# One table of steps in a new order: linear attention and a gated projection on one core

## The chip, the core and the metric

The kernel runs on one core of one Trainium2 chip, in one launch. The metric is the device time of one execution in microseconds (us); a figure for a kernel is the median of three timed runs. The engines of the core are named as in the profile: PE (TensorE, the matrix products), PEld (its weight loads), DVE (VectorE), ACT (ScalarE), POOL (GpSimd) and SP (SyncE, which issues the transfers).

## The reference

There are 8 batches of 8 heads, 576 tokens and 64 features. The first half is linear attention, the second a projection with a gate from a convolution over time:

```python
q_s = exp(q - max(q, -1));  q_s = q_s / (sum(q_s, -1) + 1e-09)   # over features
k_s = exp(k - max(k, 2));   k_s = k_s / (sum(k_s, 2) + 1e-09)    # over tokens
kv  = einsum('bhsd,bhse->bhde', k_s, v)
x   = einsum('bhsd,bhde->bhse', q_s, kv)      # -> [8, 576, 512]
xp  = x with 4 rows of zeros ahead of the tokens
gate = sigmoid(sum over k < 5 of conv_w[k] * xp[:, k:k+576, :])
out  = (gate * (x @ w_val)) @ w_out
```

## The kernel before, in words

Each batch goes through the same stages; steps of several batches interleave. A step is a small function with a name, a batch and mostly a slab, that is 128 of the 512 channels (0 to 3): `value 4 1` is the product with w_val of batch 4, output slab 1. A letter at the end of a step names its engine: a for ACT, v for DVE, p for POOL. Steps without a letter have a fixed engine.

- **k.** `load_km`, `k_peak` (DVE, L271), `k_row` and `k_spread` (transfers) find the maximum of each channel; `k_sub` (L286) takes it off in five pieces, `k_exp` (ACT, L290 and L291) raises them. Batches 0 and 1 have k by channels (`k_top`, `k_raise`) and turn it on PE. `kv` (PE, L393) forms k'v, `kv_norm` (L403 to L411) divides, `kv_high` and `kv_low` (L419) split it into a rounded upper part and the rest.
- **q.** `q_max` (DVE, L343), `q_sub` (L347), `q_exp` (ACT, L351), `q_sum` (DVE, L358 to L360) and `q_mul` (L378 on ACT in eight small instructions, L380 elsewhere), the last three in parts. `q_turn` (PE, L425) transposes q, `q_turned` copies it, `q_low` (DVE, L435) keeps the rest.
- **x.** `attend` (PE, L458, L459) gives a slab of x in PSUM. `x_high` copies its upper part, `x_low` (DVE, L478) the rest; `first` (L472 on ACT, L474 on DVE) and four `tap` steps build the gate from the same PSUM tile. A tap is one instruction on DVE (L484), or a product on ACT (`far`, L487) and a sum on POOL (L488). `sigmoid` (ACT, L491) ends the gate.
- **products.** `value` (PE, L502) multiplies all four slabs of x with one slab of w_val, 24 matmuls with upper and lower parts; `gated` (DVE, L523) makes g, `g_high` and `g_low` (L531) split it; `project` (PE, L502) does the same with w_out, and `store` copies the result from PSUM and sends it out (L545).
- **weights.** `part`, `field`, `scaled`, `signed`, `joined`, `w_high` and `w_low` turn the 64-bit words of w_val (slabs 0 to 3) and w_out (4 to 7) and of the taps (8) into upper and lower parts of 32 bits.

What sets the order is written out by hand: the table ORDER (lines 32 to 134) holds 893 steps, and a loop calls them one after the other. Each engine works off its own steps in this order and waits, in order, for what they need; nothing is moved by a planner. The PSUM tiles come from two pools of two buffers each: `x` (x and the turned q) and `mm` (kv, values, products). So the third tile of a pool waits until one of the two before it has been read for the last time: an `attend` waits for the taps and `x_low` of an earlier one, a `project` for a `store`. `warm 0` issues nothing.

Of the kernel before, what the change touches and what calls it, by code (L numbers as in the profile page):

```python
# [47 lines left out]
    attend 0 2, w_high 3 a, w_low 3 p, first 0 2 a, tap 0 2 3 v, w_high 2 a, tap 0 2 2 a, x_high 0 2 a, attend 0 3,
    load_km 2 1, warm 0, first 0 3 a, signed 4, x_high 0 3 a, w_low 2 p, kv_norm 1 a, part 4 a, sigmoid 0 0,
    x_low 0 2, x_low 0 3, value 0 0, load_q 2, scaled 5 a, load_v 2, tap 0 3 3 v, q_mul 1 0 p, tap 0 2 1 v,  # L50
    q_mul 1 3 p, tap 0 3 2 v, tap 0 2 0 v, joined 4 p, gated 0 0, value 0 2, k_peak 2 1, sigmoid 0 2, tap 0 3 1 v,
    g_high 0 0 a, gated 0 2, value 0 1, w_high 4 a, q_mul 1 1 p, sigmoid 0 1, signed 5, g_high 0 2 a, field 7,
    load_km 2 0, field 6, q_turn 1 0, g_low 0 2 v, g_low 0 0 p, value 0 3, tap 0 3 0 v, part 5 a, q_max 2, w_low 4 p,
    sigmoid 0 3, load_km 2 3, gated 0 1, k_peak 2 0, q_turned 1 0 a, joined 5 p, q_turn 1 1, w_high 5 p, scaled 6 a,
    w_low 5 p, gated 0 3, scaled 7 a, q_turned 1 1 a, k_peak 2 3, g_high 0 1 a, g_high 0 3 a, attend 1 0, attend 1 1,
    first 1 0 a, signed 7, first 1 1 a, x_high 1 0 a, signed 6, q_sub 2 2 p, g_low 0 3 v, q_sub 2 0 p, g_low 0 1 p,
    tap 1 0 3 v, part 6 a, tap 1 0 2 v, project 0 0, load_q 3, joined 6 p, tap 1 1 3 a, x_low 1 0, w_high 6 a,
    x_high 1 1 a, project 0 1, warm 0, tap 1 0 1 v, tap 1 0 0 v, k_row 2, attend 1 3, load_k 3, w_low 6 p,
    load_km 3 0, q_sub 2 3 v, part 7 a, load_km 3 1, tap 1 1 2 v, q_sub 2 4 p, store 0 0 a, tap 1 1 1 v, store 0 1 a,
    project 0 2, joined 7 p, k_spread 2, tap 1 1 0 v, first 1 3 a, x_low 1 1, x_high 1 3 a, w_high 7 a, q_sub 2 1 p,  # L60
    attend 1 2, sigmoid 1 1, store 0 2 a, w_low 7 p, k_sub 2 0 p, sigmoid 1 0, project 0 3, q_max 3, x_high 1 2 a,
    k_sub 2 3 p, tap 1 3 3 v, x_low 1 3, k_sub 2 1 p, tap 1 3 2 v, x_low 1 2, k_peak 3 1, k_sub 2 2 p, load_km 4 2,
    q_exp 2, first 1 2 a, tap 1 3 1 v, value 1 0, store 0 3 a, q_sum 2, gated 1 0, tap 1 2 3 v, load_km 3 3,
    k_peak 3 3, k_sub 2 4 p, value 1 1, k_peak 3 0, q_mul 2 4 p, load_v 4, k_exp 2, load_km 3 2, gated 1 1,
    q_mul 2 3 p, kv 2, tap 1 3 0 v, q_mul 2 0 a, sigmoid 1 3, g_high 1 0 p, g_low 1 0 p, q_mul 2 1 p, value 1 3,
    tap 1 2 2 v, kv_norm 2 a, q_mul 2 2 p, k_peak 3 2, kv_high 2 a, tap 1 2 1 v, q_turn 2 0, q_turned 2 0 a,
    load_km 4 0, k_row 3, g_high 1 1 a, tap 1 2 0 v, q_sub 3 1 p, sigmoid 1 2, gated 1 3, q_sub 3 3 p, kv_low 2 p,
    g_low 1 1 p, k_peak 4 0, q_turn 2 1, g_high 1 3 a, tail_turn 2, warm 0, q_sub 3 2 p, q_turned 2 1 v, g_low 1 3 p,
    q_low 2 0, value 1 2, tail_turned 2 a, k_spread 3, q_low 2 1, gated 1 2, attend 2 1, g_high 1 2 p, first 2 1 v,
    g_low 1 2 p, tap 2 1 3 v, q_sub 3 0 p, load_q 4, k_sub 3 0 p, attend 2 0, project 1 3, k_peak 4 2, x_high 2 0 a,  # L70
    k_sub 3 1 p, first 2 0 a, k_sub 3 3 p, load_k 4, load_km 5 1, tap 2 1 2 v, load_km 4 3, load_km 5 3, tap 2 1 1 v,
    project 1 1, q_exp 3, load_v 3, x_high 2 1 a, k_sub 3 2 p, x_low 2 0, tap 2 0 3 v, k_peak 5 1, store 1 3 a,
    load_km 4 1, store 1 1 a, x_low 2 1, project 1 0, k_sub 3 4 p, warm 0, tap 2 1 0 a, tap 2 0 2 v, tap 2 0 1 v,
    attend 2 2, k_exp 3, store 1 0 a, tap 2 0 0 a, first 2 2 a, kv 3, q_sum 3, x_high 2 2 a, attend 2 3, k_peak 4 1,
    first 2 3 a, q_max 4, q_mul 3 1 p, tap 2 3 3 a, project 1 2, q_mul 3 3 p, kv_norm 3 v, k_peak 5 3, tap 2 2 3 v,
    kv_high 3 p, tap 2 3 2 a, x_low 2 2, x_high 2 3 a, q_mul 3 2 p, load_km 7 3, q_sub 4 1 p, x_low 2 3, tap 2 2 2 v,
    q_sub 4 0 p, sigmoid 2 1, tap 2 2 1 v, load_km 5 0, value 2 1, k_peak 4 3, kv_low 3 v, store 1 2 a, q_mul 3 0 a,
    tap 2 2 0 v, load_km 6 3, value 2 2, sigmoid 2 2, q_turn 3 0, gated 2 1, tap 2 3 1 v, q_sub 4 3 p, q_turned 3 0 a,
    gated 2 2, tap 2 3 0 v, k_row 4, q_low 3 0, g_high 2 2 a, q_sub 4 2 p, load_v 6, value 2 0, k_peak 6 3,
    g_high 2 1 a, sigmoid 2 0, g_low 2 2 v, q_turn 3 1, load_q 5, gated 2 0, attend 3 0, q_sub 4 4 p, k_spread 4,  # L80
    q_turned 3 1 a, sigmoid 2 3, first 3 0 v, q_low 3 1, load_km 6 2, g_low 2 1 p, tap 3 0 3 v, value 2 3, q_exp 4,
    g_high 2 0 p, g_low 2 0 p, x_high 3 0 a, gated 2 3, attend 3 1, k_peak 5 0, load_km 5 2, g_high 2 3 v,
    tap 3 0 2 v, first 3 1 a, x_low 3 0, tap 3 0 1 v, load_kt 4, k_peak 6 2, g_low 2 3 p, x_high 3 1 a, tap 3 1 3 a,
    tap 3 1 2 a, x_low 3 1, tap 3 0 0 v, project 2 3, k_sub 4 3 v, project 2 0, attend 3 3, q_sum 4, tap 3 1 1 a,
    store 2 3 a, k_peak 5 2, k_sub 4 0 p, tap 3 1 0 a, x_high 3 3 a, k_sub 4 4 p, warm 0, k_sub 4 1 p, sigmoid 3 0,
    attend 3 2, first 3 2 a, k_sub 4 2 v, store 2 0 a, x_high 3 2 a, project 2 1, x_low 3 2, tap 3 2 3 v, tap 3 2 2 v,
    q_mul 4 3 p, k_row 5, project 2 2, store 2 1 a, first 3 3 v, q_mul 4 0 a, tap 3 2 1 a, x_low 3 3, sigmoid 3 1,
    tap 3 3 3 a, load_km 7 0, value 3 0, store 2 2 v, q_mul 4 1 p, q_max 5, gated 3 0, q_mul 4 4 p, tap 3 3 2 v,
    load_km 6 0, k_spread 5, tap 3 2 0 v, value 3 1, tap 3 3 1 v, k_exp 4, tap 3 3 0 v, q_mul 4 2 a, q_sub 5 3 p,
    kv 4, gated 3 1, kv_norm 4 v, q_turn 4 0, g_high 3 0 v, k_sub 5 4 p, sigmoid 3 2, q_turn 4 1, sigmoid 3 3,  # L90
    q_sub 5 1 v, tail_turn 4, load_k 5, q_turned 4 0 a, q_sub 5 0 p, g_low 3 0 p, k_peak 6 0, load_km 6 1,
# [523 lines left out]
```

## Time and profile before

| | |
|---|---|
| median of 3 runs | 320.69 us (319.01 to 322.22) |
| profiled execution, its own time | 319.41 us |
| its span in the trace | 317.4 us |
| granted TensorE clock | 1.00 |
| PE, PEld busy | 283.7 us (89%), 270.6 us (85%) |
| DVE, ACT, POOL busy | 266.2 us (84%), 221.8 us (70%), 210.1 us (66%) |
| chain that ended last | PE 65%, DVE 26%, issue 3%, DMA 2%, others 1% or less each |
| DMA | 51.26 MB, 161 GB/s |

The span runs from the first to the last instruction that the profiler shows; the profiled execution's own time holds some 2.0 us more around it. The busy share of an engine is a mean over stages. The chain is followed back from the last instruction, at each step to what released it. In the timeline, a row is one instruction or a run of like ones (x24) with its start and its length in us, and in brackets the time that the engine stood idle before it and what ended that.

### The profile page before, as it was taken

How to read it: one execution, taken by the hardware profiler on the slowest of the kernel's cores; microseconds unless marked ns; L12 is line 12 of the kernel's file. 1: busy time of each engine (PE TensorE's matmuls, PEld its weight loads, DVE VectorE, ACT ScalarE, POOL GpSimd, SP SyncE). 2: the span in 40 equal slices, each digit the busy share in tenths (PEclk: the TensorE clock that was granted, in tenths of full speed). 3: DMA queues.
4: the chain of work that ended last, by engine and by line, in shares of the span. 5: the costliest groups of instructions: out<-in, count | busy, mean ns of one | idle time of the engine just before them, and what ended most of it. 6: DMA issues, size and time to landing. Idle time of an engine off the chain costs nothing.

```text
span 317.4 us, 6412 instructions
## 1 busy us (share of the span) xinstructions
PE 283.7 (89%) x2512; PEld 270.6 (85%) x2512; DVE 266.2 (84%) x347; ACT 221.8 (70%) x377; POOL 210.1 (66%) x183
## 2 busy tenths in 40 slices
...
DMA packets 20526, 51.26 MB, mean 161 GB/s; under 512 B 2832, under 2 KB 7312, under 8 KB 17808
## 3 DMA queue, kind: packets, MB, share of 16 engines
...
q8 instruction: 20, 0.33, 0.4%
q14 instruction: 10, 0.08, 0.1%
HBM read 41.39 MB, written 9.45 MB: 160 GB/s over the span
## 4 chain that ended last, share of the span: by engine, by line
PE 65%; DVE 26%; issue 3%; DMA 2%; SPq 1%; ACT 1%; POOL 0%; DVEq 0%; ACTq 0%
PE val L502 29%; PE out L502 22%; PE x L458 5%; PE kv L393 5%; DVE gate L484 4%; DVE qm L343 4%; PE qTps L425 3%; DMA q<-in_q_tail 2%; DVE gl L531 2%; DVE e L237 2%; DVE qs L358 2%; DVE xl L478 2%; DVE g L523 1%; DVE kpk L271 1%; DVE qTlo L435 1%
## 5 line engine op out<-in xcount | busy, mean ns | idle before, releaser
L488 POOL TENSOR_TENSOR gate<-gate,far 128x572 f32<-128x572 f32 (+3 forms) x40 | 52.9, 1324 | 35.8 <-ACT far L487 34.9
L484 DVE SCALAR_TENSOR_TENSOR gate<-x,cw,gate 128x573 f32<-128x573 f32 (+3 forms) x88 | 70.6, 810 | 3.0 <-POOL gate L488 1.6
L502 PE MATMUL out<-gh,w_out_lo 128*128 128x288 f32 x256 | 57.1, 302 | 0.6 <-ACT o L158 0.6
L502 PE MATMUL val<-xh,w_val_lo 128*128 128x288 f32 x256 | 56.4, 301 | 0.4 <-issue 0.4
L502 PE MATMUL out<-gl,w_out_hi 128*128 128x288 f32 x256 | 55.6, 296 | 0.9 <-DVE gl L531 0.9
L502 PE MATMUL out<-gh,w_out_hi 128*128 128x288 f32 x256 | 55.5, 295 | 0.0
L502 PE MATMUL val<-xl,w_val_hi 128*128 128x288 f32 x256 | 54.8, 295 | 0.0
L502 PE MATMUL val<-xh,w_val_hi 128*128 128x288 f32 x256 | 54.8, 295 | 0.0
L502 PEld LDWEIGHTS out<-gl,w_out_hi 128*128 128x128 f32 x256 | 41.4, 188 | 1.1 <-DVE gl L531 1.1
L487 ACT ACTIVATE far<-x,cw 128x572 f32<-128x572 f32 (+3 forms) x40 | 28.9, 741 | 19.1 <-DVE gate L484 10.3
L502 PEld LDWEIGHTS val<-xh,w_val_lo 128*128 128x128 f32 x256 | 40.9, 188 | 1.2 <-issue 0.6
L502 PEld LDWEIGHTS out<-gh,w_out_lo 128*128 128x128 f32 x256 | 41.1, 189 | 0.8 <-ACT o L158 0.8
L502 PEld LDWEIGHTS out<-gh,w_out_hi 128*128 128x128 f32 x256 | 41.5, 188 | 0.0
L502 PEld LDWEIGHTS val<-xl,w_val_hi 128*128 128x128 f32 x256 | 41.2, 188 | 0.2 <-DVE xl L478 0.2
L502 PEld LDWEIGHTS val<-xh,w_val_hi 128*128 128x128 f32 x256 | 41.4, 188 | 0.0
L531 POOL TENSOR_TENSOR gl<-g,gh 128x576 fp32r<-128x576 f32 x22 | 31.8, 1445 | 9.7 <-ACT gh L158 5.3
L523 DVE TENSOR_TENSOR g<-val,gate 128x576 f32<-128x576 f32 x32 | 24.0, 752 | 15.8 <-PE val L502 14.6
L158 ACT COPY o<-out 128x576 f32<-128x576 f32 (+1 forms) x24 | 15.0, 627 | 18.3 <-PE out L502 18.0
L347 POOL TENSOR_TENSOR q<-q,qm 128x512 f32<-128x512 f32 x23 | 25.5, 1125 | 3.3 <-DVE qm L343 2.4
L286 POOL TENSOR_TENSOR k<-k,kmax 128x512 f32<-128x512 f32 x20 | 26.4, 1346 | 1.2 <-DMA kmax<-krow 1.2
L491 ACT ACTIVATE gate<-gate 128x576 f32<-128x576 f32 x32 | 21.5, 682 | 8.3 <-DVE gate L484 8.1
L315 PE MATMUL kps<-ident,kc 128*128 128x128 f32 x32 | 5.8, 349 | 20.8 <-ACT q L371 20.0
...
## 6 DMA issues: line engine op xcount, KB each, us to landing
...
```

Of the source, the lines that this page charges most:

```text
L158: nc.scalar.copy(out=out, in_=in_)
L286: engine(e).tensor_sub(kk[r, cs], kk[r, cs], mx[r, cs])
L347: engine(e).tensor_sub(qq, qq, T["qm", b][:, cs].unsqueeze(2).broadcast_to([P, H, D]))
L393: nc.tensor.matmul(acc[h * D:(h + 1) * D, p, :], T["k", b][:, c, cs] if c < 4 else ktz[b % 2][:, cs], T["v", b][:, c, hd] if c < 4 else T[ ...
L458: nc.tensor.matmul(ps[:, :MAIN], a, z, start=(i == 0), stop=(i == len(parts) - 1))
L484: nc.vector.scalar_tensor_tensor(out=a, in0=x, scalar=w, in1=a, op0=ALU.mult, op1=ALU.add)
L487: nc.scalar.activation(part, x, AF.Copy, scale=w)
L488: nc.gpsimd.tensor_add(a, a, part)
L491: nc.scalar.activation(T["gate", b, p], T["gate", b, p], AF.Sigmoid)
L502: nc.tensor.matmul(ps[:, cs], a[:, kb, ms], z[kb][:, cs], start=(kb == 0 and i == 0), stop=(kb == NB - 1 and i == 2),)
L523: nc.vector.tensor_mul(T["g", b, m], T["val", b, m], T["gate", b, m])
L531: engine(e).tensor_sub(T["gl", b, m], T["g", b, m], T["gh", b, m].bitcast(F32))
```

## The change

The table holds the same 893 steps in another order, and 141 of them end in another letter, so that they run on another engine. Nothing but the table differs, and every step with a fixed engine stays where it was. By kind, the steps of each engine before and now:

| step | ACT | DVE | POOL |
|---|---|---|---|
| g_high | 16, 13 | 5, 9 | 11, 10 |
| k_sub | | 5, 8 | 25, 22 |
| q_sub | | 4, 2 | 23, 25 |
| q_mul | 10, 6 | 5, 5 | 21, 25 |
| kv_high | 2, 3 | 1, 1 | 3, 2 |
| kv_low | | 3, 0 | 3, 6 |
| q_turned | 12, 13 | 4, 3 | |
| store | 25, 28 | 9, 5 | |
| first | 23, 24 | 9, 8 | |
| tap | 40, 39 | 88, 89 | sums of those of ACT |
| part | 7, 7 | 2, 0 | 0, 2 |
| scaled | 8, 7 | 1, 0 | 0, 2 |

A few rows of the table as they stand in the diff (batch 0 in the prologue, and batches 6 and 7):

```diff
-    q_mul 0 3 v, k_top 1 3, part 0 a, load_v 1, scaled 0 v, part 2 a, load_k 2, q_mul 0 4 p, q_exps 1 0 p,
...
-    store 6 1 a, project 6 0, x_high 7 1 v, x_low 7 1, x_low 7 0, tap 7 1 0 a, tap 7 0 1 v, attend 7 2, store 6 3 a,
...
+    kv 0, q_mul 0 4 v, part 2 a, q_exps 1 3 p, part 3 p, q_mul 0 1 p, q_turn 0 0, q_exps 1 1 p, kv_norm 0 a, warm 0,
...
+    tap 7 1 0 a, x_low 7 1, attend 7 2, tap 7 0 0 v, x_low 7 0, store 6 0 a, project 6 1, store 6 3 a, attend 7 3,
```

**DVE, batch 0 ahead of the first product.** The last tap of slab 0, the first of slab 2, weights (L246, L247), the sums of kv (L403, L404), `x_low` of slabs 2 and 3, then taps. Before:

```order
L484 SCALAR_TENSOR_TENSOR gate_0_0_395<-x_0_0_383,cw_73,gate_0_0_395 128x572
L484 SCALAR_TENSOR_TENSOR gate_0_2_478<-x_0_2_473,cw_73,gate_0_2_478 128x575
L246 TENSOR_SCALAR e4_231<-e4_231 128x512
L247 SCALAR_TENSOR_TENSOR e4_231<-words4_169,e4_231 128x512
L403 TENSOR_SCALAR ks_1_500<-kv_1_431 128x4
L404 RECIPROCAL ks_1_500<-ks_1_500 128x4
L478 TENSOR_TENSOR xl_0_2_514<-x_0_2_473,xh_0_2_485 128x576
L478 TENSOR_TENSOR xl_0_3_516<-x_0_3_487,xh_0_3_497 128x576
L484 SCALAR_TENSOR_TENSOR gate_0_3_493<-x_0_3_487,cw_73,gate_0_3_493 128x575
```

and now:

```order
L484 SCALAR_TENSOR_TENSOR gate_0_0_373<-x_0_0_365,cw_73,gate_0_0_373 128x572
L484 SCALAR_TENSOR_TENSOR gate_0_2_481<-x_0_2_473,cw_73,gate_0_2_481 128x575
L246 TENSOR_SCALAR e4_353<-e4_353 128x512
L247 SCALAR_TENSOR_TENSOR e4_353<-words4_320,e4_353 128x512
L403 TENSOR_SCALAR ks_1_499<-kv_1_428 128x4
L404 RECIPROCAL ks_1_499<-ks_1_499 128x4
L478 TENSOR_TENSOR xl_0_2_510<-x_0_2_473,xh_0_2_479 128x576
L484 SCALAR_TENSOR_TENSOR gate_0_3_493<-x_0_3_486,cw_73,gate_0_3_493 128x575
L478 TENSOR_TENSOR xl_0_3_514<-x_0_3_486,xh_0_3_497 128x576
```

The first tap of slab 3 (L484 on `gate_0_3`) now stands ahead of `x_low` of slab 3, which stood ahead of it.

**ACT, around the exponentials of batch 2.** L351 is `q_exp`, L290 and L291 `k_exp`, L158 a copy (`o` a store, `xh` an `x_high`), L491 a sigmoid; a table load stands where the function changes. Before:

```order
L351 ACT_TABLE_LOAD
L351 ACTIVATE q2_543<-q2_543 128x2560
L472 ACTIVATE gate_1_2_908<-x_1_2_855,cw_73 128x576
L158 COPY o_0_3_936<-out_0_3_865 128x576
L290 ACTIVATE k2_297<-k2_297 128x2048
L291 ACTIVATE ktz0_80<-kt2_361 64x512
L378 ACTIVATE q2_543<-q2_543,qs_2_939 128x64 x8
L491 ACT_TABLE_LOAD
```

and now:

```order
L351 ACT_TABLE_LOAD
L351 ACTIVATE q2_414<-q2_414 128x2560
L158 COPY o_0_2_874<-out_0_2_834 128x576
L158 CAST xh_1_2_906<-x_1_2_864 128x576
L491 ACT_TABLE_LOAD
L491 ACTIVATE gate_1_0_720<-gate_1_0_720 128x576
L158 COPY o_0_3_917<-out_0_3_877 128x576
L290 ACT_TABLE_LOAD
L290 ACTIVATE k2_688<-k2_688 128x2048
L291 ACTIVATE ktz0_80<-kt2_158 64x512
L378 ACTIVATE q2_414<-q2_414,qs_2_910 128x64 x8
L491 ACT_TABLE_LOAD
```

The sigmoid of slab 0 now stands between the two exponentials, with a table load on each side; `first` of slab 2 stands elsewhere, and one `x_high` and one more store have come between them.

**PE, the projects of batch 6 with the attends of batch 7.** `out_6_1` is `project 6 1`, `x_7_2` is `attend 7 2`. The end of the second project and the start of the third, before:

```order
L502 MATMUL out_6_3_3415<-gh_6_3_3371,w_out_lo_77 128x288 x2
L502 MATMUL out_6_3_3415<-gh_6_3_3371,w_out_hi_76 128x288 x2
L502 MATMUL out_6_3_3415<-gl_6_3_3373,w_out_hi_76 128x288 x2
L502 MATMUL out_6_0_3452<-gh_6_0_3290,w_out_lo_77 128x288 x2
L502 MATMUL out_6_0_3452<-gh_6_0_3290,w_out_hi_76 128x288 x2
L502 MATMUL out_6_0_3452<-gl_6_0_3299,w_out_hi_76 128x288 x2
L502 MATMUL out_6_0_3452<-gh_6_1_3271,w_out_lo_77 128x288 x2
```

and now:

```order
L502 MATMUL out_6_3_3402<-gh_6_3_3311,w_out_lo_77 128x288 x2
L502 MATMUL out_6_3_3402<-gh_6_3_3311,w_out_hi_76 128x288 x2
L502 MATMUL out_6_3_3402<-gl_6_3_3360,w_out_hi_76 128x288 x2
L458 MATMUL x_7_2_3435<-qT_7_3297,kvs_7_3254 128x512 x2
L458 MATMUL x_7_2_3435<-qTlo_7_1_3342,kvs_7_3254 128x512
L459 MATMUL x_7_2_3435<-qTt_6_2913,kvd1_79 128x64
L502 MATMUL out_6_1_3446<-gh_6_0_3244,w_out_lo_77 128x288 x2
L502 MATMUL out_6_1_3446<-gh_6_0_3244,w_out_hi_76 128x288 x2
L502 MATMUL out_6_1_3446<-gl_6_0_3308,w_out_hi_76 128x288 x2
L502 MATMUL out_6_1_3446<-gh_6_1_3282,w_out_lo_77 128x288 x2
```

`attend 7 2` now stands between the second and the third product of batch 6; it stood behind the third. The third product is now `project 6 1`, and the first `project 6 0`.

## Rows read from the trace of the kernel before

**Rows 1.** The page, part 1: busy time and share of the span by engine.

```profile
PE 283.7 (89%) x2512; PEld 270.6 (85%) x2512; DVE 266.2 (84%) x347; ACT 221.8 (70%) x377; POOL 210.1 (66%) x183
```

**Rows 2.** Timeline of PE: start, length, work, and idle time before it in brackets.

```profile
50.06 0.50 PE L502 MATMUL val<-xh,w_val_lo 128*128 128x288 f32 x2 [0.43 <-issue]
...
70.43 0.54 PE L502 MATMUL out<-gl,w_out_hi 128*128 128x288 f32 x2 [0.88 <-DVE gl L531]
...
74.33 1.10 PE L458 MATMUL x<-qT,kvd 128*128 128x512 f32 x2 [0.18 <-DVE gate L484]
```

**Rows 3.** Timeline of DVE, prologue to the first projects.

```profile
48.28 0.76 DVE L478 TENSOR_TENSOR xl<-x,xh 128x576 fp32r<-128x576 f32 x1 [0.41 <-ACT xh L158]
...
52.69 0.76 DVE L523 TENSOR_TENSOR g<-val,gate 128x576 f32<-128x576 f32 x1 [0.76 <-ACT gate L491]
...
56.16 1.66 DVE L247 SCALAR_TENSOR_TENSOR e<-words,e 128x512 int32<-128x512 int32 x1
...
66.69 1.22 DVE L246 TENSOR_SCALAR e<-e 128x512 int32<-128x512 int32 x1
...
68.56 0.42 DVE L246 TENSOR_SCALAR e<-e 128x512 int32<-128x512 int32 x1
69.02 0.69 DVE L247 SCALAR_TENSOR_TENSOR e<-words,e 128x512 int32<-128x512 int32 x1
69.62 0.75 DVE L531 TENSOR_TENSOR gl<-g,gh 128x576 fp32r<-128x576 f32 x1
```

**Rows 4.** Timeline of PE, batch 4 projects with batch 5 attends.

```profile
214.47 0.42 PE L502 MATMUL out<-gl,w_out_hi 128*128 128x288 f32 x2
215.58 0.73 PE L458 MATMUL x<-qT,kvs 128*128 128x512 f32 x2 [0.69 <-ACT far L487]
```

**Rows 5.** Timeline of PE, the second and third project of batch 6.

```profile
279.18 0.43 PE L502 MATMUL out<-gl,w_out_hi 128*128 128x288 f32 x2
280.17 0.53 PE L502 MATMUL out<-gh,w_out_lo 128*128 128x288 f32 x2 [0.56 <-ACT o L158]
```

**Rows 6.** Groups by line: count, busy us, mean ns of one, idle before.

```profile
L347 POOL TENSOR_TENSOR q<-q,qm 128x512 f32<-128x512 f32 x23 | 25.5, 1125 | 3.3 <-DVE qm L343 2.4 <-issue 0.8
...
L380 POOL TENSOR_TENSOR q<-q,qs 128x512 f32<-128x512 f32 x21 | 22.0, 1054 | 3.3 <-ACT ktz L291 1.3 <-ACT ktz L158 1.1 <-DVE qs L360 0.9
...
L484 DVE SCALAR_TENSOR_TENSOR gate<-x,cw,gate 128x575 f32<-128x575 f32 x22 | 17.8, 810 | 0.4 <-ACT gate L472 0.2
...
L271 DVE TENSOR_REDUCE kpk<-km 128x1 f32<-128x576 f32 x24 | 17.7, 743 | 0.5 <-DMA km<-in_k_strided 0.4
...
L160 POOL CAST gh<-g 128x576 fp32r<-128x576 f32 x11 | 8.3, 754 | 14.2 <-DVE g L523 14.2
...
L380 DVE TENSOR_TENSOR q<-q,qs 128x512 f32<-128x512 f32 x5 | 4.2, 850 | 0.0
...
L160 POOL CAST kvs<-kvd 128x512 fp32r<-128x512 f32 x3 | 1.8, 612 | 1.2 <-DVE kvd L408 1.2
...
L166 DVE TENSOR_SCALAR e<-e 128x512 f32<-128x512 f32 x1 | 0.4, 415 | 0.0
```

**Rows 7.** One line's or tile's instructions on DVE: ns min/median/max.

```profile
L286 DVE TENSOR_TENSOR k<-k,kmax x4: 684/850/1564, 141.3 to 240.0; 128x512 f32<-128x512 f32 x4
...
L160 DVE CAST gh<-g x5: 451/459/1029, 136.8 to 302.4; 128x576 fp32r<-128x576 f32 x5
```

**Rows 8.** What POOL waited for, 62 to 90 us: total, times, longest.

```profile
POOL q L347 <- DVE qm L343: 2.4, 1, 2.4
POOL f L251 <- ACT far L487: 2.2, 1, 2.2
```

**Rows 9.** Timeline of ACT around the exponentials of batch 2.

```profile
80.71 1.28 ACT L351 ACT_TABLE_LOAD   x1
...
87.27 0.61 ACT L291 ACTIVATE ktz<-kt 64x512 f32<-64x512 f32 x1
```

**Rows 10.** Timeline of PE at kv of batch 2.

```profile
89.46 0.69 PE L393 MATMUL kv<-v,k 128*64 128x65 f32 x16
```

More of the change, by code (lines that the diff above doesn't have):

```diff
@@ L48 @@
[L48 to L91, printed above, removed]
-    g_high 3 1 v, q_low 4 0, load_q 6, q_turned 4 1 v, value 3 2, tail_turned 4 a, kv_high 4 a, kv_low 4 p, q_low 4 1,
@@ L103 @@
-    g_low 4 0 p, sigmoid 4 3, sigmoid 4 2, gated 4 2, q_turned 5 1 a, attend 5 0, q_sub 6 1 v, value 4 3,
-    g_high 4 1 a, k_peak 7 1, q_low 5 1, first 5 0 v, g_low 4 1 v, gated 4 3, g_high 4 2 p, tap 5 0 3 v, attend 5 1,
-    k_row 6, k_spread 6, k_sub 6 1 p, x_high 5 0 v, load_q 7, g_low 4 2 p, tap 5 0 2 v, x_low 5 0, g_high 4 3 p,
-    g_low 4 3 p, project 4 0, q_exp 6, project 4 2, first 5 1 a, x_high 5 1 a, tap 5 0 1 v, tap 5 0 0 v, k_peak 7 2,
-    tap 5 1 3 a, q_max 7, store 4 0 a, k_row 7, tap 5 1 2 a, k_sub 6 4 v, attend 5 2, project 4 3, sigmoid 5 0,
@@ new lines @@
+    k_sub 2 1 p, load_km 3 1, q_max 3, q_exp 2, k_sub 2 2 p, store 0 2 a, project 0 3, k_sub 2 0 p, k_sub 2 4 p,
+    x_low 1 3, x_high 1 2 a, x_low 1 2, q_sum 2, sigmoid 1 0, q_mul 2 3 p, k_peak 3 1, store 0 3 a, value 1 0,
+    gated 1 0, k_peak 3 0, k_exp 2, q_mul 2 4 p, load_km 4 0, tap 1 3 1 v, value 1 1, first 1 2 v, gated 1 1,
+    q_mul 2 1 p, q_mul 2 2 p, tap 1 3 0 v, q_mul 2 0 a, q_sub 3 3 p, kv 2, g_high 1 0 p, sigmoid 1 3, tap 1 2 3 v,
+    warm 0, kv_norm 2 a, q_sub 3 0 p, tap 1 2 2 v, kv_high 2 a, value 1 3, tap 1 2 1 v, g_high 1 1 a, g_low 1 0 p,
@@ new lines @@
+    first 3 2 v, tap 3 2 3 v, x_low 3 2, project 2 2, x_low 3 3, tap 3 2 2 v, q_mul 4 4 p, k_row 5, k_exp 4,
+    store 2 2 a, value 3 0, tap 3 3 3 v, value 3 1, q_sub 5 1 p, load_k 5, warm 0, q_sub 5 0 p, gated 3 0,
+    tap 3 3 2 v, tap 3 3 1 v, k_spread 5, tap 3 3 0 v, sigmoid 3 1, tap 3 2 1 a, gated 3 1, q_mul 4 1 p, q_sub 5 3 p,
+    g_high 3 1 p, kv 4, tail_turn 4, q_mul 4 3 a, g_low 3 1 p, sigmoid 3 3, q_turn 4 0, tap 3 2 0 v, kv_norm 4 v,
+    kv_high 4 p, tail_turned 4 v, load_km 6 1, q_turn 4 1, k_peak 6 3, g_high 3 0 v, q_turned 4 0 v, g_low 3 0 p,
```

138 lines of the change are left out of this document (89 added, 49 removed).

## The prediction

> **What bounds the kernel now.** I read the page's busy shares first, then the timeline of PE from its first product to its last, and only then the engine that each gap of PE names. PE is busy 89% of the span [rows 1], and that share hides two different kernels. From 74.33 us on, where the second attend group of batch 1 begins [rows 2], products follow each other on PE almost without a gap; the reader should see there that the distance from row to row, 0.27 us for two matmuls, does not change. Before 74.33 us PE waits for others. The wait that shows the limit best is the one at 70.43 us, 0.88 us for g_low of batch 0 on DVE [rows 2]. Its DVE row starts at 69.62 us without any idle time ahead of it [rows 3]: DVE had been working without a break, and what it did earlier decides when PE can go on. So the early part is bound by the order and length of DVE's work, the later part by PE itself.
>
> In the later part two gaps are large enough to be worth something. The attend at 215.58 us follows a pair that began at 214.47 us; with 0.27 us for that pair the gap is 215.58 - 214.47 - 0.27 = 0.84 us, and ACT's half of a tap is named as the last to release the tile [rows 4]. The third project of batch 6 starts at 280.17 us after a pair at 279.18 us: 0.72 us, for a store on ACT [rows 5]. Since PE's work is the same matmuls before and after, only three things can move the time: what DVE delivers before 74 us, these late gaps, and new gaps.
>
> **The change, part by part.**
>
> *DVE before the first project.* Ahead of g_low of slab 3, the row at 69.62 us, DVE gains q_mul 0 4 (0.85 us) and the first step of slab 0 (0.81 us, taken like a tap on the same tile), and loses part 3 and scaled 0 (0.42 us each, from the one such row) and k_peak 2 0 (0.74 us), which moves behind it [rows 6]. Sum: 0.85 + 0.81 - 0.42 - 0.42 - 0.74 = +0.08 us, nothing. What changes is DVE's waiting. It stood idle 0.41 us for an x_high and 0.76 us for a sigmoid [rows 3]. In the new order a tap of slab 3 (0.81 us [rows 6]) stands ahead of the x_low that waited, and the product that needs this x_low starts its sigmoid earlier against DVE's work. I take the two waits as mostly filled: 0.08 - 0.41 - 0.76 = -1.1 us, and say -1.0. The price is at the other end: x_low of slab 3 comes later by 0.85 + 0.81 - 0.42 - 0.42 + 0.81 - 0.41 = 1.2 us, and value 0 2 (50.06 us [rows 2]) starts later by between 0.3 and 1.2 us; that is hidden, because the project that follows waits for DVE in any case.
>
> *The first attend after it.* k_peak 2 0 now stands ahead of the taps that free the tile for attend 1 3 (74.33 us): +0.74 us. Of the -1.0 us there remains **-0.3 us**. Its bounds are -1.1 (k_peak fills a wait of DVE) and +0.7 (no wait is filled).
>
> *The late gaps.* In batch 6 attend 7 2 now stands between the second project and the third, so that ACT's store has an attend's time more. An attend's first pair of matmuls alone takes 0.73 us in the row at 215.58 us [rows 4], about the gap; it goes: -0.7 us. In batch 5 attends 5 2 and 5 3 now come together behind three projects, and the DVE steps that stand ahead of attend 5 3 in the table fall by six, 35 leaving and 29 coming, at some 0.8 us each (a tap [rows 6]). DVE should be ahead there, and the gap go: -0.8 us. Sum **-1.5 us**, between 0 (both gaps come back elsewhere) and -1.5, all of it.
>
> *What becomes tight.* Four places lose the distance that hid work: q_low 2 0 ahead of attend 2 1, value 4 0 right behind attend 4 3, q_turn 5 1 behind a tap of batch 4, and g_low 6 2 on POOL ahead of project 6 0. Each is one operation away from being late, so each costs between nothing and one such operation, 0.8 us (a tap). I take one in four: **+0.8 us**, with ends of 0 and 3.2.
>
> *Steps that change engine elsewhere.* Four stores leave DVE, six q_mul and a few others leave ACT or come to POOL. They lie beside PE's products, which cover them as long as the engine that takes them is not late; where it could be is the second rival. The table adds no wait on SP's queue that stands ahead of an earlier need: of the loads I found none close to its first reader.
>
> *A place where POOL and DVE meet.* On DVE one k_sub takes from 0.68 to 1.56 us and one g_high from 0.45 to 1.03 us [rows 7]; the same operation doubles at some times. Three more k_sub and four more g_high now run on DVE. At the medians they cost 3 x 0.85 + 4 x 0.46 = 4.4 us of DVE time, at the longest 3 x 1.56 + 4 x 1.03 = 8.8 us. I take the medians, to which most of these instructions are near. The Trainium skill, "SBUF — State Buffer", section "Who interferes with whom", says that DVE's second pair of ports is shared with GpSimd and locked for a whole instruction, and that operations with two SBUF inputs or a copy in a fast mode want it, while one that reads PSUM alone does not. By that rule the trade of stores out of PSUM for k_sub and g_high in SBUF goes against DVE, and the 4.4 us above could be nearer 8.8; the doubled rows agree with it, though no row shows which POOL instruction stood beside them.
>
> **Sum.** -0.3 - 1.5 + 0.8 = -1.0 us. The profiled execution took 319.4 us, so 318.4 us; the median of the runs stands 1.3 us above that execution (320.7 against 319.4), so the forecast on its scale is **319.7 us**.
>
> **The rivals.**
>
> *Clearly faster.* The weight conversions of DVE just ahead of the first project are stretched: 1.66 us against 0.69 us for the same line (L247), 1.22 against 0.42 us (L246) [rows 3], 1.8 us in all. In the new order they stand elsewhere, and POOL does other work beside them. If they run at their short times, DVE reaches g_low 1.8 us sooner, the late gaps go and nothing new comes: -0.3 - 1.8 - 1.5 = -3.6 us, 317.1 us on the median's scale. For it speaks that DVE has no idle time there, so that any shortening arrives; against it, that POOL gets more work in the same stretch.
>
> *Slower: POOL becomes late at kv 2.* Ahead of the last k_sub of batch 2, POOL gains q_sub 2 3 (1.13 us), two g_high (0.75 us each), part 3 and scaled 2, and loses one q_mul (1.05 us) [rows 6]. A product with a number on POOL has no row; the nearest are a cast of the same size, 0.61 us, and a subtraction, 1.13 us [rows 6]. So 1.13 + 1.51 - 1.05 + 2 x 0.61 = 2.8 us, or 3.8 us at the other end. POOL feeds k_exp 2, which ended at 87.27 + 0.61 = 87.88 us [rows 9], and kv 2 started at 89.46 us [rows 10]: a margin of 1.6 us. ACT has in addition to load the table again ahead of k_exp 2 (1.28 us [rows 9]) because a sigmoid now stands between. If POOL's waits of 2.4 and 2.2 us in that stretch [rows 8] do not shrink, kv 2 is late by 3.8 - 1.6 + 1.3 = 3.5 us, and PE with it. POOL's sums also end the taps, so that the late gaps stay. -0.3 + 3.5 + 0.8 = +4.0 us: 324.7 us. It decides once POOL takes over more than about 1.6 us of the shift. Against it: those two waits, 4.6 us together, are more than the shift.
>
> *DVE loses at the ports what it gains.* The seven moved instructions at their longest cost 4.4 us more. Half of it on the path takes the late gain back and adds a little: -1.0 + 2.2 = +1.2 us, 321.9 us.
>
> *The change does nothing.* PE's matmuls fill the stretch from 74 us on, and the early part ends where it did: 320.7 us.
>
> **Chances.** The forecast's own case 0.33, clearly faster 0.27, POOL late 0.19, ports 0.13, nothing 0.08. A measurement of this kernel can tell about 1% from no change, so faster means below 317.5 us and slower above 323.9 us. Faster takes the first rival and 0.02 of the forecast's lower edge, 0.29; slower takes POOL late and 0.02 of the ports, 0.21; the rest, 0.50, is within 1%. The range reaches down to the first rival with the k_peak bound added (317.1 - 0.8, and a little for the spread of the runs), 315.8 us, and up past the ports to the milder half of POOL late, 323.5 us. Left out are the worse half of POOL late and gains that no row shows.
>
> **What would show it.** Right: DVE's wait ahead of the x_low and g of batch 0 is gone and the stall in the first project is under 0.3 us; the attend group of batch 5 and the third project of batch 6 start without a gap; attend 1 3 starts between 73 and 74.5 us. Wrong: kv 2 waits for ACT or POOL; L246 and L247 rows near 0.4 and 0.7 us throughout (the faster case); k_sub and g_high on DVE mostly above 1 us (the ports). The sum fails if a new gap of over 1 us stands anywhere after 74 us, since nothing there makes it up: PE has no room to catch up.

## The result and the profile after

The changed kernel is slower. Twenty runs of each give 321.69 us (320.6 to 322.57) against 319.93 us (318.58 to 322.22), a ratio of 1.005 with a 95% interval of 1.0033 to 1.0067; a second set of twelve runs gave 1.0044 (1.0022 to 1.0067). The forecast was 1.0 us less; it came out 1.6 us more by the ratio and 1.8 us by the medians. The time lies inside the stated range, but on the other side of no change.

The profiled execution took 322.06 us, its span is 320.3 us, 2.9 us longer than before. Against [rows 1] DVE and ACT have less to do (262.1 and 214.9 us busy), POOL more (216.4 us), and none of it tells why the kernel is slower. PE's work is the same 2512 matmuls, so the span is split by PE's timeline. Three points carry it: attend 1 3, the start of the last four projects, and the last matmul.

| | before | after | difference |
|---|---|---|---|
| start of attend 1 3, us | 74.33 | 75.86 | +1.5 |
| from there to the start of the last four projects (301.32, 302.81) | 227.0 | 226.95 | 0.0 |
| last matmul's start to the end of the span | 317.4 - 313.96 = 3.4 | 320.3 - 315.45 = 4.9 | +1.4 |

**The first projects.** The timeline of PE after answers to [rows 2] (start, length, work, idle time before it). The reader should see the stall of 2.63 us, three times that of before, and then the length of the rows: from 71.94 us a pair takes 0.68 us instead of 0.43 us.

```profile
64.94 0.53 PE L502 MATMUL out<-gh,w_out_lo 128*128 128x288 f32 x2
...
70.77 0.54 PE L502 MATMUL out<-gl,w_out_hi 128*128 128x288 f32 x2 [2.63 <-DVE gl L531]
...
71.94 0.68 PE L502 MATMUL out<-gh,w_out_lo 128*128 128x288 f32 x2
...
75.86 1.02 PE L458 MATMUL x<-qT,kvd 128*128 128x512 f32 x2
```

The stall is longer for two reasons. PE comes to it earlier: its first product of this group, at 64.94 us above, started at 66.31 us before:

```profile
66.31 0.52 PE L502 MATMUL out<-gh,w_out_lo 128*128 128x288 f32 x2
```

That is 1.4 us of the added 1.75 us. It costs no time by itself, though the lower clock below follows the longer stall. The stall ends at 70.77 us instead of 70.43 us, 0.3 us later, and that is DVE's part.

The table of windows (length, busy us of PE, PEld, DVE, ACT, POOL, then the granted clock) shows what lengthened the rows behind it: the granted clock of PE was 0.58 there, so for most of that stretch it stood at the lower of its two levels (1.2 instead of 2.4 GHz), and the stretch ahead of it is the one in which PE did 1.37 us of work in 4.

```profile
68.00:72.00 4.00, 1.37 (x11) 1.23 (x10) 4.00 (x4) 2.19 (x4) 3.86 (x4) 0.99 0.00 2
72.00:76.00 4.00, 4.00 (x20) 4.00 (x20) 3.96 (x7) 0.00 (x0) 4.00 (x4) 0.58 0.34 84
```

So the 1.5 us at attend 1 3 have three parts. The stall ends 0.34 us later. From its end to attend 1 3 it took 3.90 us before and takes 5.09 us now; with the clock held at 1.00, in an experiment below, it takes 4.34 us. So 0.75 us are the lower clock and 0.44 us are DVE's taps, which free the tile later.

The stall ends when DVE's g_low is done. DVE's timeline after answers to [rows 3]; the wait for an x_high is now 0.52 us for a sum of POOL, the wait for a sigmoid is gone, and still g_low starts at 69.56 us, as before (69.62 us), and takes 1.16 us instead of 0.75 us:

```profile
49.01 0.82 DVE L484 SCALAR_TENSOR_TENSOR gate<-x,cw,gate 128x575 f32<-128x575 f32 x1 [0.52 <-POOL gate L488]
...
53.95 0.75 DVE L523 TENSOR_TENSOR g<-val,gate 128x576 f32<-128x576 f32 x1
...
56.00 2.65 DVE L237 TENSOR_SCALAR e<-words 128x512 f32<-128x512 f32 x2
58.58 0.41 DVE L246 TENSOR_SCALAR e<-e 128x512 int32<-128x512 int32 x1
59.02 0.69 DVE L247 SCALAR_TENSOR_TENSOR e<-words,e 128x512 int32<-128x512 int32 x1
59.63 0.75 DVE L531 TENSOR_TENSOR gl<-g,gh 128x576 fp32r<-128x576 f32 x1
...
65.21 0.96 DVE L246 TENSOR_SCALAR e<-e 128x512 int32<-128x512 int32 x1
66.21 1.41 DVE L247 SCALAR_TENSOR_TENSOR e<-words,e 128x512 int32<-128x512 int32 x1
67.55 0.41 DVE L246 TENSOR_SCALAR e<-e 128x512 int32<-128x512 int32 x1
67.99 1.64 DVE L247 SCALAR_TENSOR_TENSOR e<-words,e 128x512 int32<-128x512 int32 x1
69.56 1.16 DVE L531 TENSOR_TENSOR gl<-g,gh 128x576 fp32r<-128x576 f32 x1
```

The rows of before that [rows 3] leaves out:

```profile
55.41 0.72 DVE L246 TENSOR_SCALAR e<-e 128x512 int32<-128x512 int32 x1
...
57.74 1.85 DVE L237 TENSOR_SCALAR e<-words 128x512 f32<-128x512 f32 x2
59.51 1.16 DVE L531 TENSOR_TENSOR gl<-g,gh 128x576 fp32r<-128x576 f32 x1
...
67.95 0.69 DVE L247 SCALAR_TENSOR_TENSOR e<-words,e 128x512 int32<-128x512 int32 x1
```

Not every row grew. The weight rows and the g_low between 55 and 61 us took 5.39 us together before and take 4.50 us now; the four weight rows between 65 and 70 us took 3.02 us and take 4.42 us. The net is +0.5 us.

POOL's timeline shows what it did beside the later rows: two q_sub, a sum of weights and a cast:

```profile
64.84 2.23 POOL L347 TENSOR_TENSOR q<-q,qm 128x512 f32<-128x512 f32 x2
67.75 1.33 POOL L251 TENSOR_TENSOR f<-e,f 128x512 int32<-128x512 int32 x1 [0.68 <-ACT f L164]
69.15 0.96 POOL L160 CAST w_out_hi<-f 128x512 fp32r<-128x512 f32 x1
```

**The late stage.** The two gaps of [rows 4, 5] are gone: attends 5 2 and 5 3 follow the third project, and project 6 1 follows attend 7 2, without idle time (timeline of PE):

```profile
216.25 0.42 PE L502 MATMUL out<-gl,w_out_hi 128*128 128x288 f32 x2
216.51 0.63 PE L458 MATMUL x<-qT,kvs 128*128 128x512 f32 x2
...
282.46 0.33 PE L459 MATMUL x<-qTt,kvd 128*128 128x64 f32 x2
282.60 0.52 PE L502 MATMUL out<-gh,w_out_lo 128*128 128x288 f32 x2
```

What they gave is spent at kv 3, which had no gap in the trace of before:

```profile
113.02 0.69 PE L393 MATMUL kv<-v,k 128*64 128x65 f32 x16
113.53 0.29 PE L393 MATMUL kv<-vt,ktz 128*64 128x65 f32 x4
```

and now:

```profile
114.92 0.69 PE L393 MATMUL kv<-v,k 128*64 128x65 f32 x16 [0.37 <-ACT k L290]
116.36 0.34 PE L393 MATMUL kv<-vt,ktz 128*64 128x65 f32 x4 [0.74 <-ACT ktz L291]
```

The second row starts 1.44 us behind the first instead of 0.51 us, and with the wait ahead of the first PE loses 1.4 us here; another 0.2 us goes at an attend of batch 7, which waits for q_low. The chain of waits (start, length, work) runs through kv 3, from a maximum of batch 3 on DVE by two transfers to POOL, ACT and PE:

```profile
96.53 0.67 DVE kpk L271
...
97.21 3.17 DMA krow<-kpk
...
100.84 6.87 DMA kmax<-krow
...
107.86 5.06 POOL k L286 x4
112.92 1.38 POOL gate L488
...
114.37 1.29 POOL kt L286
...
115.67 0.64 ACT ktz L291
...
116.36 2.09 PE kv L393 x64
```

DVE's k_peak 3 2 began at 96.44 us, 3.4 us later than before (93.08 us). The spread of the maximum was issued at 100.84 us, 4.5 us later than before (96.39 us), while PE was only 1.5 us later, and it landed after 6.87 us instead of 3.2 us. POOL waited 2.71 us for it; before, it had landed some 5 us ahead of POOL's first k_sub 3.

**The end.** The timeline of ACT: all three last copies stand behind the last matmul, 1.24 us of them; before, one of 0.40 us stood there. Before:

```profile
314.29 0.40 ACT L158 COPY o<-out 128x288 f32<-128x288 f32 x1 [5.73 <-PE out L502]
```

and now:

```profile
315.82 1.24 ACT L158 COPY o<-out 128x288 f32<-128x288 f32 x3 [5.73 <-PE out L502]
```

In the table the order is project 7 3 l, project 7 2, project 7 3 r, store 7 3 l, store 7 2, store 7 3 r; before, each store stood behind its own product. This part does not vary: from the start of the last matmul to the end of the span it takes 4.84 to 4.88 us in the seven traces with the change's tail and 3.40 to 3.47 us in the seven with each store behind its product.

### The profile page after: what moved, and what is told of

The parts are those of the page before. It is cut to its first block, busy times and chain, and to the rows that moved or that the text cites. A ratio compares the mean times of both kernels' runs of the same rounds, so it can differ in the third digit from the quotient of the medians.

```text
span 320.3 us, 6383 instructions
## 1 busy us (share of the span) xinstructions
PE 286.7 (90%) x2512; PEld 274.3 (86%) x2512; DVE 262.1 (82%) x341; ACT 214.9 (67%) x347; POOL 216.4 (68%) x190
## 4 chain that ended last, share of the span: by engine, by line
PE 63%; DVE 18%; DMA 8%; POOL 3%; issue 2%; ACT 2%; SPq 1%; ACTq 0%; DVEq 0%; POOLq 0%
PE out L502 29%; PE val L502 22%; PE x L458 5%; DVE gate L484 4%; PE kv L393 4%; DMA kc<-in_k_channels 3%; DMA q<-in_q 2%; DVE qs L358 2%; PE qTps L425 2%; DMA kmax<-krow 2%; POOL k L286 2%; DVE kpk L271 1%; DVE g L523 1%; DVE q L380 1%; PE x L459 1%
## 5 line engine op out<-in xcount | busy, mean ns | idle before, releaser
L484 DVE SCALAR_TENSOR_TENSOR gate<-x,cw,gate 128x572 f32<-128x572 f32 (+3 forms) x89 | 70.8, 809 | 7.9 <-ACT gate L472 4.1
L488 POOL TENSOR_TENSOR gate<-gate,far 128x572 f32<-128x572 f32 (+3 forms) x39 | 51.9, 1333 | 26.1 <-ACT far L487 25.2
L502 PEld LDWEIGHTS out<-gh,w_out_lo 128*128 128x128 f32 x256 | 41.8, 192 | 0.4 <-POOL w_out_lo L259 0.2
L502 PEld LDWEIGHTS out<-gh,w_out_hi 128*128 128x128 f32 x256 | 42.2, 191 | 0.0
L158 ACT COPY o<-out 128x576 f32<-128x576 f32 (+1 forms) x28 | 17.1, 620 | 23.3 <-PE out L502 23.0
L380 POOL TENSOR_TENSOR q<-q,qs 128x512 f32<-128x512 f32 x25 | 26.3, 1071 | 7.6 <-DVE qs L360 7.6
L491 ACT ACTIVATE gate<-gate 128x576 f32<-128x576 f32 x32 | 21.5, 685 | 10.4 <-DVE gate L484 5.4
L347 POOL TENSOR_TENSOR q<-q,qm 128x512 f32<-128x512 f32 x25 | 26.8, 1083 | 0.7 <-PE out L502 0.7
L478 DVE TENSOR_TENSOR xl<-x,xh 128x576 fp32r<-128x576 f32 x32 | 23.7, 749 | 3.2 <-ACT far L487 2.1
```

The costliest lines, as they stand in the source:

```text
L158: nc.scalar.copy(out=out, in_=in_)
L347: engine(e).tensor_sub(qq, qq, T["qm", b][:, cs].unsqueeze(2).broadcast_to([P, H, D]))
L380: engine(e).tensor_mul(qq, qq, s.unsqueeze(2).broadcast_to([P, H, D]))
L478: nc.vector.tensor_sub(xl, T["x", b, p], T["xh", b, p].bitcast(F32))
L484: nc.vector.scalar_tensor_tensor(out=a, in0=x, scalar=w, in1=a, op0=ALU.mult, op1=ALU.add)
L488: nc.gpsimd.tensor_add(a, a, part)
```

## The experiments

Four theories stand for the loss: the tail, DVE held up by POOL ahead of the first projects, the clock behind the stall, and the late maximum of batch 3. Ratios are to the kernel before, with their 95% intervals; the quotient of two medians can differ from them by 0.15%. The changed kernel itself is at 1.005 (1.0033 to 1.0067).

The first runs of the tail, of q_sub, of the transposes and of the earlier maximum were made together, without the changed kernel, so that a gain against it is a difference between sets of runs. Such sets can differ by more than the intervals say: below, the same kernel gives 1.0084 in one and 1.0044 in another. A difference of 0.3 or 0.4% between sets counts here as shown only where the traces have it too.

**The tail alone put back.**

```diff
-    project 7 3 l, project 7 2, project 7 3 r, store 7 3 a l, store 7 2 a, store 7 3 a r,
+    project 7 3 l, store 7 3 a l, project 7 2, store 7 2 a, project 7 3 r, store 7 3 a r,
```

> The changed kernel with two of its last steps moved back: store 7 3 a l stands right behind project 7 3 l, and store 7 2 a right behind project 7 2; all on ACT as in the change. Theory (the tail): in the changed kernel the three last copies on ACT all start after the last matmul (315.82 us, 1.24 us together) where before only one of 0.40 us was left; the last matmul to the end of the span took 4.7 us against 3.3 us before. So this gains 0.8 to 1.4 us and the three copies start apart. Rival (the end is set by the last transfer alone, whatever stands before it): no change, within 0.3 us.

Measured: 1.0007 (0.9987 to 1.0026), so some 0.4% or 1.4 us better, the top of what was expected. The traces have the same 1.4 us: the copies on ACT start apart again, and the span ends 317.7 - 314.23 = 3.5 us behind the last matmul:

```profile
309.83 0.40 ACT L158 COPY o<-out 128x288 f32<-128x288 f32 x1 [0.95 <-PE out L502]
313.03 0.64 ACT L158 COPY o<-out 128x576 f32<-128x576 f32 x1 [2.80 <-PE out L502]
314.56 0.40 ACT L158 COPY o<-out 128x288 f32<-128x288 f32 x1 [0.89 <-PE out L502]
```

All three are on ACT, as in the change: the place in the order costs the time, not the engine.

**The change's tail in the kernel before.**

```diff
-    project 7 3 l, store 7 0 a, store 7 3 v l, project 7 2, store 7 2 v, project 7 3 r, store 7 3 a r,
+    project 7 3 l, store 7 0 a, project 7 2, project 7 3 r, store 7 3 a l, store 7 2 a, store 7 3 a r,
```

> The kernel before with the change's tail alone: the copies of store 7 3 l and store 7 2 move to ACT and stand behind project 7 3 r. Theory (the tail): the same loss from the other side, 1.2 to 1.7 us slower than the kernel before, 1.004 to 1.005; three copies follow the last matmul. Rival (the copies lie beside the last transfer): no change.

Measured: 1.0045 (1.0024 to 1.0067), 1.4 us slower. That is as large as the whole change. The trace ends 320.5 - 315.66 = 4.8 us behind the last matmul, 1.4 us more than before, so the tail is shown from both sides. The same trace holds a wait that the trace of before does not: PE stands 1.67 us at q_turn 2 (97.79 us), after DVE waited 2.39 us for a load of batch 3's k instead of 0.18 us. The order up to there is that of before. So an execution of the kernel before can hold such a gap too, and a gap that hangs on a transfer, as the one at kv 3, should not be sized from one pair of traces.

**POOL kept away from two of DVE's weight rows.**

```diff
-    project 0 0, part 7 a, q_sub 2 1 p, load_v 2, x_low 1 0, tap 1 0 2 v, q_sub 2 0 p, joined 6 p, w_high 6 p,
-    k_peak 2 0, load_q 3, w_low 6 p, load_km 3 3,
+    project 0 0, part 7 a, load_v 2, x_low 1 0, tap 1 0 2 v, joined 6 p, w_high 6 p,
+    k_peak 2 0, load_q 3, w_low 6 p, q_sub 2 1 p, q_sub 2 0 p, load_km 3 3,
```

> The changed kernel with q_sub 2 1 and q_sub 2 0 on POOL moved behind w_low 6, so that POOL stands idle while DVE makes signed 6 (65 to 67.5 us). Theory (DVE and POOL hold each other up): those two DVE rows take 0.41 and 0.69 us instead of 0.96 and 1.41 us, g_low 0 3 starts about 1.3 us earlier, the stall of 2.63 us in the first project shrinks by as much, and attend 1 3 starts 0.8 to 1.3 us earlier, unless the later q_sub make kv 2 late. Rival (the long rows come from DVE's own inputs): rows stay near 1 and 1.4 us, no change before 76 us.

Measured: 1.0017 (1.0002 to 1.0031), some 0.3% or 1.0 us better than the changed kernel; the trace gives 2.0 us at attend 1 3, so the size is open between the two. Nothing of DVE's order was touched; its timeline shows the first pair of weight rows at their short times, and the second long row, beside POOL's next sum (66.38 us, 1.35 us), as it was:

```profile
65.10 0.42 DVE L246 TENSOR_SCALAR e<-e 128x512 int32<-128x512 int32 x1
65.55 0.69 DVE L247 SCALAR_TENSOR_TENSOR e<-words,e 128x512 int32<-128x512 int32 x1
66.16 0.42 DVE L246 TENSOR_SCALAR e<-e 128x512 int32<-128x512 int32 x1
66.62 1.67 DVE L247 SCALAR_TENSOR_TENSOR e<-words,e 128x512 int32<-128x512 int32 x1
68.21 1.16 DVE L531 TENSOR_TENSOR gl<-g,gh 128x576 fp32r<-128x576 f32 x1
```

PE's stall shrinks, the lower clock does not appear (granted 1.00), and attend 1 3 starts 2.0 us earlier, now held by DVE's taps. Of the 2.0 us the earlier end of the stall gives 1.35 us; the rest lies behind it, where the clock is no longer low:

```profile
69.42 0.53 PE L502 MATMUL out<-gl,w_out_hi 128*128 128x288 f32 x2 [1.41 <-DVE gl L531]
...
73.86 1.10 PE L458 MATMUL x<-qT,kvd 128*128 128x512 f32 x2 [0.70 <-DVE gate L484]
```

The Trainium skill, "SBUF — State Buffer", section "Who interferes with whom", gives a rule that fits: the ports that DVE shares with GpSimd are locked for a whole instruction, and DVE operations with two SBUF inputs, beside a GpSimd operation that reads SBUF, or in a two-port mode want them. The rows that stretch here read SBUF; the taps, x_low and 128x576 copies, which have an input in PSUM, stay at 0.73 to 0.82 us in the whole trace of the changed kernel. The experiment shows that POOL's place lengthens the rows; that it does so by the ports is not shown.

**PE kept at work in the stall.**

```diff
-    first 1 0 a, project 0 1, tap 1 0 3 v,
+    first 1 0 a, warm 24, project 0 1, tap 1 0 3 v,
```

> The changed kernel with 24 transposes of the identity (some 2.4 us of PE's time) ahead of project 0 1, so that PE works where it stood idle for 2.63 us; DVE's order is the same. Theory (the clock): the granted clock of 0.58 in 72 to 76 us follows from that idle time. Without it the products behind the stall run at 0.27 us a pair instead of 0.48 us, and attend 1 3 starts at about 75.0 us, where DVE's taps let it, instead of 75.86: 0.8 us gained. Rival 1 (DVE alone sets attend 1 3): no change, though the clock reads 1.00. Rival 2 (the clock falls for another reason): still near 0.6 in that stretch.

Measured: 1.0084 (1.0071 to 1.0097), with four runs. The mechanism shows as expected: granted clock 1.00 in 72 to 76 us, the stall down to 0.38 us, attend 1 3 at 74.94 us. The time does not follow. Both kernels were then run side by side:

> The changed kernel with 24 transposes ahead of project 0 1, run again beside the changed kernel, since its first four runs (322.15 us) did not show the 0.8 us that its trace did. Theory (the clock costs 0.8 us behind the stall): 0.5 to 1.0 us faster than the changed kernel of this call. Rival (whatever PE saves there is lost outside the products): equal to it or slower.

> The changed kernel itself, unchanged, as the base for the kernels of this call. All theories: about 1.005 of the kernel before, that is some 1.6 us slower. Its trace says whether the gap at kv 3 (1.5 us in the first trace, 0.4 us in the trace of the kernel with the tail moved) differs from execution to execution with the landing time of the spread maximum.

Measured: 1.0044 (1.0025 to 1.0063) for it, 1.0044 (1.0022 to 1.0067) for the changed kernel. In these two traces attend 1 3 starts at 75.64 and 75.94 us. The stall of the first ends 0.4 us later than that of the second for reasons ahead of it; from the end of the stall to attend 1 3 both traces with transposes take 4.34 us, and the four with the lower clock 5.08 to 5.10 us. So the lower clock costs 0.75 us at this place. In the time this is not to be seen: intervals of 0.2%, some 0.6 us each way, can just miss it, and in these two traces PE waits at kv 3 until 115.98 and 115.86 us, so that what came before is used up there. The clock is not shown as a cause of the longer time. The trace of the changed kernel here has the kv 3 gap again, 0.8 us on PE, with POOL waiting 2.11 us for the maximum.

**The maximum of batch 3 earlier.**

```diff
-    load_k 3, tap 1 2 0 v, load_km 5 3, k_peak 3 2, q_turn 2 0, q_turned 2 1 a, k_row 3,
+    load_k 3, k_spread 3, tap 1 2 0 v, load_km 5 3, q_turn 2 0, q_turned 2 1 a,
...
-    gated 1 0, k_peak 3 0, k_exp 2,
+    gated 1 0, k_peak 3 0, k_peak 3 2, k_row 3, k_exp 2,
```

> The changed kernel with k_peak 3 2 moved up to behind k_peak 3 0, k_row 3 right behind it (ahead of load_k 3 on SP's queue), and k_spread 3 right behind load_k 3. Theory (late maximum): k_sub 3 waits 2.71 us for the spread maximum (107.86 us), this makes k_exp 3 late and kv 3 with it, 1.5 us on PE. With the maximum earlier POOL starts k_sub 3 at about 105 us and the gaps at kv 3 (0.37 and 0.74 us in the waits) go: 1.0 to 1.6 us gained. Rival (POOL is late by its own work, the tap sum ahead of the last k_sub): the wait for the transfer goes, kv 3 still waits for k_exp, less than 0.4 us gained.

Measured: 1.0047 (1.0032 to 1.0061), no difference that the interval can tell. The trace shows the gap gone: the spread is issued at 93.89 us, POOL does not wait and starts k_sub 3 at 105.15 us, kv 3 runs without idle time. PE's last matmul came 1.6 us earlier than in the first trace of the changed kernel, 1.1 us earlier than in the second. The size of the gap differs between executions (1.4 us in the first trace, 0.8 us in the second, 0.3 us in the trace with the tail put back), so one trace over-stated it. A loss of time at kv 3 is seen in traces and not shown in the time.

**All three edits, and two of them.** The edits are those above.

> The changed kernel with three edits at once: the last stores behind their own products, q_sub 2 1 and 2 0 behind w_low 6, and k_peak 3 2, k_row 3 and k_spread 3 earlier. Theory (three separate losses hide the gain of the late stage): the edits add up, 1.4 + 1.5 + 0.4 to 1.4 us, 317.5 to 318.5 us or 0.993 to 0.996 of the kernel before, so faster than both. Rival (PE or DVE takes back what one edit gives): no faster than the kernel before, 0.998 or more.

> The changed kernel with two of the three edits, the tail and the q_sub, without the earlier maximum of batch 3. Theory (late maximum, worth 0.4 to 1.5 us): 0.995 to 0.998 of the kernel before, against 0.9927 with all three, and a wait at kv 3 for k_exp 3. Rival (the maximum's landing costs little in most executions): 0.993 to 0.994.

Measured: 0.9927 (0.9899 to 0.9956) with all three, from six runs (medians of 318.32 us against 320.24 us, a quotient of 0.994); 0.996 (0.994 to 0.9981) with the tail and the q_sub. So the losses do hide a gain: with them undone the new order is faster than the kernel before. In the trace of all three PE waits for little from 62 us on (waits of PE: engine, line, what for, total, times, longest):

```profile
PE out L502 <- DVE gl L531: 1.4, 1, 1.4
PE x L458 <- DVE gate L484: 0.7, 1, 0.7
...
```

The third edit is worth the difference of two ratios whose intervals overlap, 0.3%, so it may be worth nothing. In the trace with two edits kv 3 loses 0.3 us, and the first project's stall ends 1.1 us later than with three (70.40 against 69.31 us), at a place that the third edit does not touch.

**attend 7 2 put back**, on top of the three edits, behind the third project of batch 6.

```diff
-    x_low 7 1, attend 7 2, tap 7 0 0 v, x_low 7 0, store 6 0 a, project 6 1, store 6 3 a, attend 7 3,
+    x_low 7 1, tap 7 0 0 v, x_low 7 0, store 6 0 a, project 6 1, store 6 3 a, attend 7 2, attend 7 3,
```

> The kernel with the three edits, and attend 7 2 put back behind the third project of batch 6, beside attend 7 3, as it stood before the change. Theory of the prediction (the attend in between covers ACT's store): a gap of 0.5 to 0.9 us comes back ahead of the third project, now project 6 1, and the time grows by as much, to 0.995 of the kernel before. Rival (the store is early enough now, since other steps around it moved too): no gap, no change.

Measured: 0.994 (0.9918 to 0.9962), no difference from 0.9927. The rival holds: no gap ahead of project 6 1. ACT's timeline shows that the copy is early enough. The store is done at 278.0 us, and the third project starts at 278.66 us:

```profile
276.73 0.74 ACT L487 ACTIVATE far<-x,cw 128x572 f32<-128x572 f32 x1 [0.69 <-POOL gate L488]
277.37 0.63 ACT L158 COPY o<-out 128x576 f32<-128x576 f32 x1
```

Before, that copy ran at 279.48 us behind two products of taps, which waited for DVE's taps, which stood behind a g_low that waited 0.76 us for POOL and then took 1.97 us. That g_low, g_low 6 3, is on POOL now. So the attend in between is not the reason for the gain; that DVE's shorter way is the reason is read from the traces, and no run moves g_low 6 3 alone.

**DVE's order ahead of the first project.** On top of the three edits, signed 7 moves behind tap 1 0 0 on DVE, and w_low 7 ahead of q_sub 2 3 on POOL. The first try also moved w_high 7 ahead of the stores on ACT:

```diff
-    x_high 1 0 a, signed 7, g_low 0 3 v,
+    x_high 1 0 a, g_low 0 3 v,
...
-    tap 1 0 0 v, x_high 1 1 a, joined 7 p,
+    tap 1 0 0 v, signed 7, x_high 1 1 a, joined 7 p,
...
-    store 0 1 a, store 0 0 a, q_sub 2 3 p,
+    w_high 7 a, store 0 1 a, store 0 0 a, w_low 7 p, q_sub 2 3 p,
```

> The kernel with the three edits (0.9927 of the kernel before), and in addition signed 7 on DVE moved behind tap 1 0 0, w_high 7 up on ACT and w_low 7 up on POOL ahead of q_sub 2 3. Theory (DVE's order alone sets the end of the first project and attend 1 3): g_low 0 3 starts about 2 us earlier, attend 1 3 at about 72 us instead of 73.75 us, and 1.5 to 2 us are gained, 0.986 to 0.989, unless project 0 3 has to wait for w_low 7. Rival (POOL's weights are next): PE waits for w_out_lo ahead of project 0 3 and kv 2 gets late with q_sub 2; less than 0.5 us gained.

Measured: 1.0031 (1.0009 to 1.0054). The stall in the first project is gone, but w_high 7 waited 6.13 us on ACT and held back both stores, so project 0 2 waited 3.92 us for its bank. The second try had w_high 7 behind both stores:

> The kernel with the three edits (0.9927), with signed 7 on DVE behind tap 1 0 0 and w_low 7 on POOL ahead of q_sub 2 3, but w_high 7 on ACT behind store 0 0 instead of ahead of both stores (there it held back store 0 1 and with it the bank for project 0 2, a wait of 3.92 us). Theory (DVE's order sets attend 1 3): attend 1 3 about 2 us earlier than with the three edits, no wait for a store, 0.5 to 1.5 us gained, 0.988 to 0.991. Rival (POOL is next): the gain at attend 1 3 is lost again at project 0 3 or kv 2, 0.992 or more.

Measured: 0.9949 (0.9928 to 0.9971). Attend 1 3 starts at 71.36 us, 2.4 us earlier than with the three edits, and PE gives it back in the next steps (waits of PE from 62 us on):

```profile
PE x L458 <- DVE gate L484: 1.3, 2, 1.1
PE val L502 <- ACT o L158: 1.0, 1, 1.0
...
```

That is the rival's outcome, no gain, with DVE and ACT as the next waits rather than POOL. The lowest ratio of all is that of the three edits; with attend 7 2 put back, or signed 7 moved, the time can't be told from it.

## Why the prediction was wrong, by its own steps

Two terms failed above all: the stores that change engine, put at nothing, cost 1.4 us at the end, and DVE's waits before the first project, put at -1.0 us, gave nothing there.

- **What bounds the kernel:** right in the main. DVE's g_low ends the stall in the first project, PE sets the late part, and what was lost at attend 1 3 was not made up.
- **DVE before the first project, -1.0 us:** wrong. g_low 0 3 starts at 69.56 us against 69.62 us. Half of the miss is the waits: the two shrank from 1.17 us to one of 0.52 us, and not to nothing, because the tap that should fill them itself waited for a sum of POOL. The other half is the rows: the sum was made with instruction times of the old order, and the weight rows with the earlier g_low took 0.5 us more in all, the four between 65 and 70 us 1.4 us more. g_low 0 3 itself grew from 0.75 to 1.16 us. Moving two POOL steps away gave 1.3 us of DVE's time back. The forecast of a stall under 0.3 us also left out that PE would come 1.4 us earlier. The first rival saw the mechanism in part: its two long rows are short now in one place, but rows of the same lines are long in another, and the three L246 and L247 pairs take 5.5 us as against 5.4 us.
- **The lower clock:** no term. It costs 0.75 us between the stall and attend 1 3 in the traces.
- **The k_peak step, +0.74 us:** in place as said, at 0.44 us. In the trace with the clock at 1.00 attend 1 3 waits 0.61 us for DVE's taps, behind that k_peak, against 0.18 us before.
- **The late gaps, -1.5 us:** both gone, 0.84 and 0.72 us, so the size was right. The reason given for batch 6 was wrong: without the attend in between the gap stays away, so the right size there was luck. The reason for batch 5, fewer DVE steps ahead of attend 5 3, was not tested.
- **What becomes tight, +0.8 us at four named places:** the size was near by luck, since none of the four came; the only wait of that kind is 0.2 us for q_low of batch 7. The loss in the trace was at kv 3, 1.4 us, through two transfers of the maximum: the gap of over 1 us behind 74 us that the prediction names as the sign of its failure. It had put such a loss at kv 2 and at POOL's own work; kv 2 had no gap. It looked at the loads' margins and not at the chain k_peak, k_row, k_spread. How much of this is in the time stays open, between nothing and 1.4 us.
- **Stores that change engine, nothing:** wrong, and the largest single miss, 1.4 us. PE's products cover a store only while there is a product left. The last three stores moved behind the last product, and the last line of the table shows it.
- **The port rival** named k_sub and g_high on DVE. Most of those stayed short (k_sub at a median of 0.68 us, g_high at 0.46 us, one of them at 1.68 us); it was the weight rows that stretched beside POOL.

Sum of what the runs showed: tail +1.4, first projects +1.5 in the trace (1.0 by the q_sub experiment), kv 3 between 0 and +1.4, late gaps about -1.6: between +0.8 and +2.7 us, against 1.4 to 1.8 us measured.
